# Down-projection weights loaded in rows of 3 KB, up-projection weights read with a column step of three

## The chip, the cores and the metric

The kernel runs on one core of one Trainium2 chip. The metric is the device time in microseconds of one execution. A second execution is recorded by the hardware profiler; its page and its trace are read here.

## What is computed

The reference is a chunked state-space layer (Mamba2 SSD) whose output goes through a bilinear feed-forward layer. Cut to what matters:

```python
# x (4, 8, 768, 32), a (4, 8, 768), B and C (4, 8, 768, 16), all float32; chunk = 32
for c in range(nc):
    cum = np.cumsum(log_a[chunk c], axis=-1)
    M = (Cc @ Bc.T) * exp(cum_i - cum_j) * causal
    y[chunk c] = M @ xc + (Cc @ state) * exp(cum)
    state = exp(sum(la)) * state + sum_j exp(cum_last - cum_j) * Bc[j] (x) xc[j]

X = y.transpose(0, 2, 1, 3).reshape(3072, 256)
out = ((X @ w_a) * (X @ w_b)) @ w_out     # w_a, w_b (256, 1536), w_out (1536, 256)
```

In the bilinear layer the order of the 1536 hidden columns is free, as long as w_a, w_b and the rows of w_out use the same order.

## The kernel before

The sequence of 768 is cut into 6 blocks of Q = 128. Two batches form a pair, so there are NP = 12 pairs of 256 tokens, numbered p = 2 * block + half of the batches. The order of instructions is written out by hand (a manual schedule): each engine runs its own instructions in the order of the Python calls, and the framework adds the semaphore waits that the tiles' reads and writes need. It finds these by comparing the regions that two instructions touch.

For each pair, the attention half does this: `scale` turns B, C and x into f16 with the decay factors (GpSimd, in the beginning VectorE and ScalarE); `transposes` brings B and C to the other orientation; `scores` forms C B in PSUM; `mask` (L319, VectorE) multiplies by the causal mask; `pv` (L328 and L362) adds the part within the block and the part from the state; ScalarE writes the result as f16 to X2T (L374); `state` carries the state on.

The feed-forward half of a pair is six calls of `unit(p, k2)`, each for two of the NK = 12 groups of 128 hidden columns. A unit does four products of `Wa` into one PSUM bank and four of `Wb` into another (L433): two column groups k by two halves f of the 256 inputs. The stationary operand is a 128 x 128 piece of the weights, the moving one is X2T of the pair (256 columns). ScalarE then copies the first bank (asb, L442), and VectorE multiplies it with the second into hk (L443). `out_half(p, bt)` is twelve products of hk with `Wo` (L450), an evacuation and a store of 128 x 256 floats.

All of TensorE's work is in one queue. The first units of up products, unit(0,0), unit(0,1) and unit(0,2), stand between the scores of pair 1 and pv(1). On VectorE the masks of pair 1 and the products hk of pair 0 alternate:

```python
    mask(product(1, 3), by_pool=True)
    for t in range(3):
        load_wo(t)
    h = unit(0, 0)
    mask(product(1, 0))
    h()
    mask(product(1, 1))
    h = unit(0, 1)
    scale_x(1, nc.scalar)
    h()
    mask(product(1, 2))
    go((0, 2))
```

The weights are loaded on GpSimd's queue, with a cast from f32 to f16 during the transfer. `Wa` and `Wb` are tiles of 128 x 2 x 1536; `load_w(half)` (L136) loads columns 0 to 767 or 768 to 1535 of both f of each. Half 0 is issued ahead of everything else on that queue, half 1 after the factors of pair 1; the first unit that uses half 1 is unit(0,3). `load_wo(t)` (L142) loads four of the twelve 128-row groups of w_out, 1 KB rows, one row of each group to a partition. Its three calls stand behind pair 1's mask on GpSimd; behind them stand hr, hs and hsx (L541 to L543), from which TensorE (L552) makes the decays G of the states.

Of the kernel before, what the change touches and what calls it, by code (L numbers as in the profile page):

```python
# [22 lines left out]
def kernel(  # L23
# [13 lines left out]
    nc = tc.nc  # L37
# [43 lines left out]
    Wo = big.tile([128, NK, d_model], f16, name="Wo")  # L81
# [56 lines left out]
        ]  # L138

    def load_wo(t):  # L140
        k = slice(4 * t, 4 * t + 4)
        nc.gpsimd.dma_start(Wo[:, k], moe_w_out.rearrange("(k p) e -> p k e", p=128)[:, k])  # L142

    nc.sync.dma_start(a_sb, a.rearrange("b h (k q) -> (b h) k q", q=Q))
    for p_ in range(3):
# [151 lines left out]
    def product(p, m):  # L297

        return (
            st[p]["T1"][:, 2 * m : 2 * m + 2].rearrange("p e r q -> p e (r q)"),  # L300
            SC[m].rearrange("p (e c) -> p e c", e=2),
        )
# [8 lines left out]
    def mask(out_in, by_pool=False):  # L311
        o_, i_ = out_in
        c_ = causal.rearrange("p r q -> p (r q)").unsqueeze(1).broadcast_to((128, 2, 2 * Q))
        if by_pool:
            tmp = mid.tile([128, 2, 2 * Q], f32, name="tmp", tag="tmp")
            nc.scalar.copy(tmp, i_)
            nc.gpsimd.tensor_tensor(out=o_, in0=tmp, in1=c_, op=ALU.mult)
        else:
            nc.vector.tensor_tensor(out=o_, in0=i_, in1=c_, op=ALU.mult)  # L319
# [103 lines left out]
    def unit(p, k2):  # L423
        s = st[p]
        if k2 == 0:
            s["hk"] = ffh.tile([128, NK, 2 * Q], f16, name="hk", tag="hk")
        a_ps = psf.tile([128, 512], f32, name="aps", tag="ff")
        b_ps = psf.tile([128, 512], f32, name="bps", tag="ff")
        for ps, W in ((a_ps, Wa), (b_ps, Wb)):
            for kk in range(2):  # L430
                k = 2 * k2 + kk
                for f in range(2):
                    nc.tensor.matmul(  # L433
                        ps[:, kk * 2 * Q : (kk + 1) * 2 * Q],
                        W[:, f, k * 128 : (k + 1) * 128],
                        X2T[:, p, f].rearrange("p t q -> p (t q)"),
                        start=(f == 0),
                        stop=(f == 1),
                        skip_group_check=True,
                    )  # L440
        asb = ffh.tile([128, 512], f32, name="asb", tag="asb")
        nc.scalar.copy(asb, a_ps)  # L442
        return lambda: nc.vector.tensor_tensor(  # L443
            out=s["hk"][:, 2 * k2 : 2 * k2 + 2, :].rearrange("p k q -> p (k q)"), in0=b_ps, in1=asb, op=ALU.mult
        )
# [35 lines left out]
    def go(*items):  # L481
        for p, k2 in items:
            unit(p, k2)()
# [43 lines left out]
    v = factors_mm(1, NBLK)  # L527
    nc.scalar.copy(flat(fC, 1, NBLK), v)
    mask(product(1, 3), by_pool=True)
    for t in range(3):  # L530
        load_wo(t)
    h = unit(0, 0)
    mask(product(1, 0))
# [5 lines that stand above are left out]
# [118 lines left out]
```

## Time and profile before

| | |
|---|---|
| device time, median of 3 runs | 134.03 us (132.4 to 134.34) |
| the profiled execution | 132.39 us, span 130.7 us |
| TensorE products (PE) | 122.9 us busy, 94% |
| TensorE weight loads (PEld) | 101.4 us, 78% |
| VectorE (DVE) | 87.3 us, 67% |
| ScalarE (ACT) | 74.5 us, 57% |
| GpSimd (POOL) | 53.5 us, 41% |
| up products, L433 | 576 of 273 ns |
| their weight loads, L433 | 576 of 98 ns |
| down products, L450 | 288 of 273 ns |
| Wo loads, L142 | 3 of 256 KB, 6.2 us from issue to landing (median) |
| mean granted TensorE clock | 0.997 |

The span is the time from the first to the last instruction of the profiled execution; its own device time is 1.7 us more. Products are pipelined: records of 273 ns overlap, so the pace of a series is read from the starts and not from the mean duration. In a line of groups the numbers after the bar are the busy time and the mean of one in ns, then the engine's idle time ahead of them. A line of the timeline has start and duration in us, engine, line, operation, and in square brackets the idle time before it with what ended it. In the chain, TensorE holds 87% of the span.

### The profile page before, as it was taken

To read this page: it belongs to the slowest core of one execution; us is meant where nothing else is said; L and a number is where in the kernel's file an instruction comes from. 1 tells how busy PE (TensorE), PEld (TensorE's weight loads), DVE (VectorE), ACT (ScalarE), POOL (GpSimd) and SP (SyncE) were. 2 spreads that over 40 slices of the span, in tenths; PEclk is the share of its full clock that TensorE was granted. 3 is DMA by queue.
4 is the path that set the end of the run, shared out by engine and by line. 5 is a ranking of instruction groups with operands and counts; after the bars stand their busy time and mean duration, and the time that the engine had idled before them with its cause. 6 is when DMAs were issued, how large, how long until landed. Compare 5 with 4: busy or idle time off the path is not lost.

```text
span 130.7 us, 4724 instructions
## 1 busy us (share of the span) xinstructions
PE 122.9 (94%) x1948; PEld 101.4 (78%) x1948; DVE 87.3 (67%) x161; ACT 74.5 (57%) x153; POOL 53.5 (41%) x76
## 2 busy tenths in 40 slices
PE   6998949989999999999999999999999999999990
PEld 2333938878888888888888888888898888888880
DVE  2786476876693974974975956957939929835441
ACT  3135645795548548556576476576575486455520
POOL 6495486547459607508409319129037000000000
PEclk9999999999999999999999999999999999999998
DMA  3999999931666561542532443614511010110112
GB/s 68 182 122 227 187 189 189 166 89 42 105 138 129 134 148 46 98 105 54 98 100 67 68 111 74 127 50 88 117 46 40 19 60 11 40 40 5 40 40 80
DMA packets 43333, 12.22 MB, mean 94 GB/s; under 512 B 37552, under 2 KB 43216, under 8 KB 43312
## 3 DMA queue, kind: packets, MB, share of 16 engines
q1 hardware_dynamic: 38256, 8.84, 32.4%
q0 software_dynamic: 2800, 2.63, 13.1%
q10 hardware_dynamic: 2256, 0.46, 1.8%
q8 instruction: 15, 0.25, 0.8%
q14 instruction: 6, 0.05, 0.2%
HBM read 11.13 MB, written 3.15 MB: 109 GB/s over the span
## 4 chain that ended last, share of the span: by engine, by line
PE 87%; ACT 5%; DVE 3%; DMA 2%; issue 1%; DVEq 0%
PE aps L433 24%; PE ops L450 23%; PE bps L433 23%; PE SC L286 4%; PE SC L328 3%; PE SC L265 2%; ACT bt L272 2%; PE SC L362 2%; PE tc L195 2%; DMA a_sb<-in_a_dram 2%; PE fps L217 1%; PE SC L345 1%; PE SC L195 1%; DVE t L319 1%; ACT X2T L374 1%
## 5 line engine op out<-in xcount | busy, mean ns | idle before, releaser
L443 DVE TENSOR_TENSOR hk<-bps,asb 128x512 f16<-128x512 f32 x72 | 49.6, 689 | 26.3 <-ACT asb L442 23.8
L442 ACT COPY asb<-aps 128x512 f32<-128x512 f32 x72 | 42.2, 587 | 18.8 <-PE aps L433 17.1
L433 PE MATMUL aps<-X2T,Wa 128*128 128x256 f16 x288 | 43.3, 273 | 0.0
L433 PE MATMUL bps<-X2T,Wb 128*128 128x256 f16 x288 | 43.2, 273 | 0.0
L450 PE MATMUL ops<-Wo,hk 128*128 128x256 f16 x288 | 35.2, 273 | 0.0
L319 DVE TENSOR_TENSOR t<-SC,causal 128x512 f16<-128x512 f32 x46 | 30.3, 682 | 1.6 <-ACT osb L465 0.8
L433 PEld LDWEIGHTS <-Wb 128*128 128x128 f16 x288 | 28.2, 98 | 3.2
L433 PEld LDWEIGHTS <-Wa 128*128 128x128 f16 x288 | 27.2, 98 | 3.9
L450 PEld LDWEIGHTS <-hk 128*128 128x128 f16 x288 | 27.7, 98 | 3.1
L408 POOL TENSOR_TENSOR sbd<-U,maskbd 128x512 f16<-128x512 f32 x10 | 11.6, 1158 | 33.2 <-DVE U L401 31.8
L465 ACT ACTIVATE osb<-ops 128x256 f32<-128x256 f32 x23 | 8.8, 384 | 16.7 <-PE ops L450 16.7
L241 POOL TENSOR_SCALAR x<-xn 128x512 f16<-128x512 f32 x9 | 13.4, 1491 | 1.1 <-DMA xn<-in_x_dram 0.4
L374 ACT ACTIVATE X2T<-SC 128x512 f16<-128x512 f32 x11 | 6.6, 597 | 7.4 <-PE SC L345 6.4
L272 ACT ACTIVATE bt<-SC,ch 128x256 f16<-128x256 f16 x22 | 9.2, 473 | 0.1
L247 POOL TENSOR_TENSOR cm<-cn,fC 128x256 f16<-128x256 f32 x11 | 6.8, 620 | 3.4 <-DMA cn<-in_C_dram 3.4
L401 DVE SCALAR_TENSOR_TENSOR U<-SC,G,gU 128x64 f32<-128x64 f32 x16 | 3.8, 280 | 5.3 <-ACT X2T L374 5.3
L286 PEld LDWEIGHTS <-bt 32*64 32x64 f16 x384 | 3.8, 108 | 4.2 <-issue 3.1
L247 POOL TENSOR_TENSOR bm<-bn,fB 128x256 f16<-128x256 f32 x11 | 6.8, 621 | 0.1
L286 PE MATMUL SC<-ct,bt 32*64 32x128 f16 x384 | 5.4, 227 | 1.3 <-ACT ct L273 1.2
L328 PEld LDWEIGHTS <-x 64*32 64x32 f16 x384 | 3.1, 91 | 4.0 <-issue 2.0
L195 PE MATMUL SC<-warm 128*128 128x512 f16 x10 | 4.8, 629 | 1.2 <-DVE warm L159 1.2
L328 PE MATMUL SC<-t,x 64*32 64x128 f16 x352 | 4.6, 218 | 1.2 <-DVE t L319 1.2
(60 smaller groups left out, 70.6 us busy)
## 6 DMA issues: line engine op xcount, KB each, us to landing
out_dram<-osb SPq DMA_DIRECT2D x23, 128.0 KB, 1.7
xn<-in_x_dram SPq DMA_DIRECT2D x21, 128.0 KB, 3.3
bn<-in_B_dram SPq DMA_DIRECT2D x24, 64.0 KB, 3.0
cn<-in_C_dram SPq DMA_DIRECT2D x21, 64.0 KB, 2.9
Wa<-in_moe_w_a_dram POOLq DMA_DIRECT2D x2, 384.0 KB, 6.1
Wb<-in_moe_w_b_dram POOLq DMA_DIRECT2D x2, 384.0 KB, 7.5
Wo<-in_moe_w_out_dram POOLq DMA_DIRECT2D x3, 256.0 KB, 6.2
xn<-in_x_dram POOLq DMA_DIRECT2D x2, 128.0 KB, 6.9
```

The costliest lines, as they stand in the source:

```text
L241: eng.tensor_scalar(xo, xi, XS, None, ALU.mult)
L247: eng.tensor_tensor(out=m_, in0=pair_in[p][which].rearrange("p h r n -> p r h n"), in1=f[:, blk, :, bp].unsqueeze(3).broadcast_to((128, 2, ...
L272: nc.scalar.activation(out=o_, in_=TB, func=AF.Copy, scale=par[:, e : e + 1])
L286: nc.tensor.matmul(SC[m][64 * bt : 64 * bt + 64, c0 : c0 + Q], BT[rows, e, r, bt], CT[rows, bt], start=True, stop=True, skip_group_check=True,
L319: nc.vector.tensor_tensor(out=o_, in0=i_, in1=c_, op=ALU.mult)
L328: nc.tensor.matmul(py[bt][32 * g : 32 * g + 32, u * Q : (u + 1) * Q], s["X16"][k, h, r, :], s["T1"][k, h, r, :], start=(first and u == 0 a ...
L408: nc.gpsimd.tensor_tensor(out=Sbd.rearrange("p t (m c) -> p t m c", m=4), in0=U32[:, p].unsqueeze(2).broadcast_to((128, 2, 4, 2 * D)), in1 ...
L433: nc.tensor.matmul(ps[:, kk * 2 * Q : (kk + 1) * 2 * Q], W[:, f, k * 128 : (k + 1) * 128], X2T[:, p, f].rearrange("p t q -> p (t q)"), sta ...
L442: nc.scalar.copy(asb, a_ps)
L443: return lambda: nc.vector.tensor_tensor(out=s["hk"][:, 2 * k2 : 2 * k2 + 2, :].rearrange("p k q -> p (k q)"), in0=b_ps, in1=asb, op=ALU.mult)
L450: nc.tensor.matmul(o_ps[:, 0:d_model], hk[:, k, bt * Q : (bt + 1) * Q], Wo[:, k, :], start=(k == 0), stop=(k == NK - 1), skip_group_check= ...
L465: nc.scalar.activation(out=o_sb, in_=o_ps[:, 0:d_model], func=AF.Copy, scale=1.0 / (YS * YS))
```

## The change

Two things change together. The load of w_out takes three consecutive rows to a partition, 3 KB in one piece, in groups of 384 rows; two transfers of six row groups replace three of four. Partition p of slot k then holds row 384 * (k // 3) + 3 * p + k % 3 of w_out. For hidden column and row to match, the up products take as stationary operand every third column of a group of 384, beginning at k % 3, in place of 128 consecutive columns. The loads of Wa and Wb and all other instructions stay as they were.

```diff
     def load_wo(t):
-        k = slice(4 * t, 4 * t + 4)
-        nc.gpsimd.dma_start(Wo[:, k], moe_w_out.rearrange("(k p) e -> p k e", p=128)[:, k])
+        k = slice(6 * t, 6 * t + 6)
+        nc.gpsimd.dma_start(
+            Wo[:, k].rearrange("p (g kk) e -> p g (kk e)", kk=3),
+            moe_w_out.rearrange("(g p kk) e -> p g (kk e)", p=128, kk=3)[:, 2 * t : 2 * t + 2],
+        )
...
                     nc.tensor.matmul(
                         ps[:, kk * 2 * Q : (kk + 1) * 2 * Q],
-                        W[:, f, k * 128 : (k + 1) * 128],
+                        W[:, f, k // 3 * 384 : (k // 3 + 1) * 384].rearrange("p (c kk) -> p kk c", kk=3)[:, k % 3],
                         X2T[:, p, f].rearrange("p t q -> p (t q)"),
...
-    for t in range(3):
+    for t in range(2):
         load_wo(t)
```

## The prediction, made before the changed kernel had run

> **What bounds the kernel now.** I read the page first (busy shares, the chain that ended last, the costliest groups), then the timeline from 5 to 24 us, then the answers on the weight tiles.
>
> ```profile
> span 130.7 us, 4724 instructions
> PE 122.9 (94%) x1948; PEld 101.4 (78%) x1948; DVE 87.3 (67%) x161; ACT 74.5 (57%) x153; POOL 53.5 (41%) x76
> ...
> PE 87%; ACT 5%; DVE 3%; DMA 2%; issue 1%; DVEq 0%
> ...
> L433 PE MATMUL aps<-X2T,Wa 128*128 128x256 f16 x288 | 43.3, 273 | 0.0
> L433 PE MATMUL bps<-X2T,Wb 128*128 128x256 f16 x288 | 43.2, 273 | 0.0
> L450 PE MATMUL ops<-Wo,hk 128*128 128x256 f16 x288 | 35.2, 273 | 0.0
> ```
>
> TensorE is the chain: 87% of the span, busy 94%. The 864 big products run without gaps from about 20 us on; four of them take 0.44 us in the chain, 109 ns each. So there are two ways to move the time: change what one of these products costs, or open a gap in TensorE's queue. The stage before 20 us, where DMA is busy throughout (tenths 9 in seven slices of the page, 3.3 to 26 us), is where gaps are.
>
> The change touches exactly the first unit of up products there, so these lines of the timeline carry the argument:
>
> ```profile
> 9.73 0.74 POOL L136 DMA_DIRECT2D Wa<-in_moe_w_a_dram  x1
> 10.47 0.74 POOL L136 DMA_DIRECT2D Wb<-in_moe_w_b_dram  x1
> ...
> 14.02 0.61 PE L433 MATMUL aps<-X2T,Wa 128*128 128x256 f16 x4
> ...
> 14.47 0.60 PE L433 MATMUL bps<-X2T,Wb 128*128 128x256 f16 x4
> ...
> 15.43 0.69 DVE L443 TENSOR_TENSOR hk<-bps,asb 128x512 f16<-128x512 f32 x1 [1.73 <-ACT asb L442]
> ...
> 17.23 0.68 DVE L319 TENSOR_TENSOR t<-SC,causal 128x512 f16<-128x512 f32 x1
> ...
> 17.97 0.42 PE L328 MATMUL SC<-t,x 64*32 64x128 f16 x32 [1.15 <-DVE t L319]
> ```
>
> The reader is to see the chain unit(0,0) -> hk -> three more DVE operations back to back -> pv(1) at 17.97. The second halves of Wa and Wb are issued at 9.73 and 10.47. The answers on tiles Wa and Wb, restricted to 9 to 12 us, give their landing, counted from issue:
>
> ```profile
> DMA to landing us min/median/max: 7.0/7.0/7.0
> ```
>
> ```profile
> DMA to landing us min/median/max: 8.3/8.3/8.3
> ```
>
> So Wa's second half lands at 9.73 + 7.0 = 16.73 us, Wb's at 10.47 + 8.3 = 18.77 us. In the kernel before nobody notices: the first product that needs them is unit(0,3), after 23 us, and TensorE has no wait on a DMA in the list of waits.
>
> **What the skill says.** The Trainium skill, "SBUF — State Buffer", section "Specifications (TRN2)": cachelines are 16 bytes and two hits per line are needed for full bandwidth. A step of three f16 elements is 6 bytes, two or three hits per line, so by the page the new stationary read runs at full rate. "TensorE: Matmul & The Clock Gate", section "Weight-path perf modes — Fast Weight Load (FWL) and DoubleRow": fast loading takes 128 non-fp32 columns in chunks "packed or strided", with column steps up to 1,024 elements. The trace of before has no strided stationary operand, so it neither confirms nor denies either. The same page, Part 1: TensorE runs at half clock until it has been busy for about 3.4 us and again after an idle window of that length. The trace agrees that there are two speeds: warm-up matmuls of 512 columns came three in 1.46 us at 4.64 us and three in 0.81 us at 11.02 us.
>
> **Part 1, the Wo load.** Three issues of 256 KB become two of 384 KB on POOL (770 ns each, 16.09 to 18.41), so POOL saves 0.77 us, and there are 512 rows of 3 KB where there were 1536 of 1 KB. What follows on POOL is hr, hs, hsx (end 19.19), read by the gps product at 19.45. But gps also stands behind ds_mm(0), released only at 19.27 by X2T on ACT, so the saving ends in a wait. The earlier landing of Wo is worth nothing either: Wo lands by 17.6 + 8.0 = 25.6 us at the latest, its first reader is at 28.80. If that cover were gone the gain would still be at most the 0.26 us between 19.19 and 19.45. Gain: 0.
>
> **Part 2, the stationary step of 3.** 576 weight loads change. A load's record is 98 ns, a product's pace 109 ns. The record isn't the occupancy: the four L362 products (contiguous 128x128 weights, 128 columns) take 0.38 us of records of 219 ns, that is (380 - 219)/3 = 54 ns apart, so a contiguous load needs at most 54 ns of its turn. Under a 256-column product there are 109 ns, so the strided load is free up to twice that. Lower bound 0 (a load cannot become shorter to any profit, it is hidden already). Upper bound: three times as many lines, three times 54 = 162 ns, 53 ns exposed x 576 = 30 us. I take 0, since the page keeps the rate and the cover is 2x.
>
> **Part 3, a wait that the diff does not show.** The compiled order of TensorE's instructions is the same in both, but two semaphore waits sit elsewhere. DMASW5 and DMASW6 are the second halves of Wa and Wb. Before, they are waited for at the first product of unit(0,3) (rows 474 and 482). In the changed kernel, at the second weight load (f = 1) of each half of unit(0,0):
>
> ```
> 249 L436 Ldweights Wa [waits DMASW1]
> 250 L436 Matmult aps<-X2T,Wa 128x256 [waits PE]
> 251 L436 Ldweights Wa [waits DMASW5]
> ...
> 257 L436 Ldweights Wb [waits DMASW2]
> 258 L436 Matmult bps<-X2T,Wb 128x256 [waits PE]
> 259 L436 Ldweights Wb [waits DMASW6]
> ```
>
> The data read are those of the first half; the strided view with f = 1 is evidently taken as overlapping the second-half write (which spans both f). So TensorE issues the first aps product at 14.02, then stands until 16.73; does the other three aps products (0.33 us) and the first bps one; then stands until 18.77. All of TensorE is queued behind: the rest of unit(0,0), unit(0,1), unit(0,2), pv(1).
>
> The step sum: the bps load at 18.77, its product at 18.88, two more at 109 ns, the last starts at 19.10 and ends, with a record of 273 ns, at 19.37; hk about 0.04 later, the lag seen between other products and their reader (20.39 to 20.43 for asb): 19.41. Before it started at 15.43. Delay 3.98 us. The copy asb of this unit, which released hk before, is done by about 17.9 now. Behind hk stand, on DVE in order, t, hk, t; they ran back to back for 2.5 us and still do, because unit(0,1) (another 0.87 us of products plus a 0.59 us copy) is ready at about 20.3, before DVE asks at 20.6. So pv(1), at 17.97, goes to 21.95, and the unbroken TensorE stretch behind it moves as a whole. Nothing later gives it back: between 20 and 127 us TensorE's waits in the profile sum to 0.5 us. DMA before 18.8 us is the same in both kernels (Wo is issued at 16.09 either way, behind the weights on the same queue), so the landing should hold to some 0.5 us.
>
> Sum: 0 + 0 + 3.98 = +4.0 us. The profiled execution took 132.39 us for a span of 130.7, so 136.4 on its terms. It lay at the low end of 132.4 to 134.34; on the median of 134.03 it is 138.0.
>
> **Rivals.**
> A. The stall also cools TensorE. From 14.3 to 18.8 us it would be busy for only some 0.5 us, in gaps of 2.5 and 1.6 us. For: the two speeds above, and the kernel's own warm-up products. Against: no single gap is 3.4 us. The following products would then take twice 109 ns for one window of about 3.4 us: half of that window is lost, 1.7 us, perhaps up to 3 with the gaps at 16 to 19 us in it: 138.0 + 1.7 to 3, about 140.3.
>
> B. The strided load doesn't fit. For: nothing in the trace shows one. Against: the 54 ns above. At 130 ns a load it costs 21 x 576 = 12 us on top (150); at 162 ns 30 us (168).
>
> C. Not slower by what can be told. The place is the idle time of the same stage: TensorE idles 1.15 us ahead of pv(1) and 0.73 us ahead of ds_mm(0). If DVE and ACT used the stall to get ahead, those gaps would close and 3.98 - 1.15 - 0.73 = 2.1 us would remain, 136.1, within 2%. It decides if the masks t of pair 1 run before hk(0,0). Against: DVE takes its instructions in order, and both t stand behind hk(0,0). A landing of Wb before 17.5 us has the same effect; earlier than 14.5 us the time would even be unchanged, 134.0.
>
> D. Faster: the Wo rows free the saturated DMA and something waits less. Part 1 bounds that at 0.26 us, 133.8. It needs the wait of part 3 not to bind.
>
> **How the numbers follow.** Forecast (138.0, within 136.4 to 139): 0.57. A: 0.20. B: 0.11. C: 0.10. D: 0.02. Two per cent is 2.7 us, about what a measurement of this kernel can tell from no change. Slower: forecast, A and B, 0.88; same: C and half of D, 0.11; faster 0.01. The range leaves out B and half of C: 135.6 to 141.5.
>
> **What would show it.** In the changed profile: TensorE waiting in unit(0,0) on DMA Wa and Wb, about 2.5 and 1.6 us; hk's first instance near 19.4; pv(1) near 22; up products still 109 ns apart; weight-load records of the up products anywhere from 98 to about 130 ns without effect; Wo's landing earlier and unread. Wrong if no DMA wait stands there, if the products' pace rises (B), or if the products after the stall show records well over 273 ns (A).

## The result, and the profile after

The changed kernel takes 137.89 us (137.62 to 138.02), the kernel before 134.04 us (132.4 to 134.34) beside it: a ratio of 1.031, 95% interval 1.023 to 1.040. Executions of the kernel before lie mostly near 132.2 or near 134.1 us, so that its median hangs on how many of each were drawn (134.04 of 4 here, 132.46 to 133.51 of 27 to 55 in the comparisons below), and the ratios are therefore ratios of means without the executions more than 1.5% above the fastest of their kernel. Against the lower ones the 3.9 us here are about 5.7 us.

The page after, in the same rows as before (its line numbers are three higher: L433 is L436):

```profile
span 135.9 us, 4723 instructions
...
PE 124.3 (91%) x1948; PEld 105.2 (77%) x1948; DVE 87.3 (64%) x161; ACT 74.6 (55%) x153; POOL 52.7 (39%) x75
...
PE 81%; DMA 9%; POOL 3%; ACT 2%; issue 1%; SPq 1%; DVE 0%; POOLq 0%
...
L436 PE MATMUL aps<-X2T,Wa 128*128 128x256 f16 x288 | 44.8, 279 | 2.9 <-DMA Wa<-in_moe_w_a_dram 2.9
L436 PE MATMUL bps<-X2T,Wb 128*128 128x256 f16 x288 | 44.5, 278 | 1.1 <-DMA Wb<-in_moe_w_b_dram 1.1
L453 PE MATMUL ops<-Wo,hk 128*128 128x256 f16 x288 | 35.2, 273 | 0.0
L436 PEld LDWEIGHTS <-Wa 128*128 128x128 f16 x288 | 29.2, 105 | 6.2 <-DMA Wa<-in_moe_w_a_dram 3.1
```

TensorE has fallen from 87% to 81% of the chain, and DMA has risen from 2% to 9%. In the groups, aps and bps had no idle time before; now they have 2.9 us that ended with DMA Wa and 1.1 us that ended with DMA Wb. The down products keep 273 ns and no idle time. The means of 279 and 278 ns for the up products are the first sign that some of them ran slower than 273. A weight load of the up products is 105 ns in the mean, 98 before.

The timeline after shows the place:

```profile
13.76 0.29 PE L436 MATMUL aps<-X2T,Wa 128*128 128x256 f16 x1
...
15.84 1.48 POOL L142 DMA_DIRECT2D Wo<-in_moe_w_out_dram  x2
...
16.97 0.82 PE L436 MATMUL aps<-X2T,Wa 128*128 128x256 f16 x3 [2.92 <-DMA Wa<-in_moe_w_a_dram]
...
17.59 0.42 PE L436 MATMUL bps<-X2T,Wb 128*128 128x256 f16 x1
...
19.11 0.82 PE L436 MATMUL bps<-X2T,Wb 128*128 128x256 f16 x3 [1.10 <-DMA Wb<-in_moe_w_b_dram]
...
19.73 1.06 PE L436 MATMUL aps<-X2T,Wa 128*128 128x256 f16 x4
20.04 0.69 DVE L446 TENSOR_TENSOR hk<-bps,asb 128x512 f16<-128x512 f32 x1 [6.60 <-PE bps L436]
...
20.58 1.06 PE L436 MATMUL bps<-X2T,Wb 128*128 128x256 f16 x4
...
23.09 0.42 PE L331 MATMUL SC<-t,x 64*32 64x128 f16 x32
...
24.90 0.62 PE L436 MATMUL aps<-X2T,Wa 128*128 128x256 f16 x4
```

One aps product at 13.76, then nothing until 16.97; three aps and one bps product, then nothing until 19.11. hk starts at 20.04 (15.43 before), pv(1) at 23.09 (17.97). And the products are slow: four take 0.85 us from start to start (19.73 to 20.58), 213 ns each and not 109. TensorE's clock has dropped, as a stretch of 2 us shows (busy us of PE, PEld, DVE, ACT, POOL, then TensorE's clock, here 0.50, the DMA share and GB/s):

```profile
20.00:22.00 2.00, 2.00 (x11) 1.45 (x10) 1.54 (x3) 1.11 (x2) 0.00 (x0) 0.50 1.19 219
```

The trace's record of the granted clock has it at half from 15.93 to 22.76 us. It fell 1.9 us after the first gap began. By 24.90 a series of four has its old 0.62 us.

The answers on Wa and Wb, restricted to 9 to 12 us, give the landing of the second halves, from issues at 9.8 and 10.6 us:

```profile
DMA to landing us min/median/max: 7.1/7.1/7.1
```

```profile
DMA to landing us min/median/max: 8.5/8.5/8.5
```

Wa is there at 16.9, Wb at 19.1 us, the moments at which TensorE goes on. TensorE waits for data that it doesn't read: unit(0,0) uses columns 0 to 383, which are all in the first half.

### The profile page after: what moved, and what is told of

It reads as the page before. It is cut to its first block, busy times and chain, and to the rows that moved or that the text cites. A ratio compares the mean times of both kernels' runs of the same rounds, so it can differ in the third digit from the quotient of the medians.

```text
span 135.9 us, 4723 instructions
## 1 busy us (share of the span) xinstructions
PE 124.3 (91%) x1948; PEld 105.2 (77%) x1948; DVE 87.3 (64%) x161; ACT 74.6 (55%) x153; POOL 52.7 (39%) x75
## 4 chain that ended last, share of the span: by engine, by line
PE 81%; DMA 9%; POOL 3%; ACT 2%; issue 1%; SPq 1%; DVE 0%; POOLq 0%
PE aps L436 24%; PE bps L436 24%; PE ops L453 22%; DMA Wb<-in_moe_w_b_dram 6%; PE SC L331 3%; PE SC L289 3%; DMA bn<-in_B_dram 3%; PE SC L268 2%; PE SC L365 2%; PE SC L348 1%; POOL Wa L136 1%; ACT bt L275 1%; ACT X2T L377 1%; POOL xn L122 1%; POOL Wb L136 1%
## 5 line engine op out<-in xcount | busy, mean ns | idle before, releaser
L436 PE MATMUL aps<-X2T,Wa 128*128 128x256 f16 x288 | 44.8, 279 | 2.9 <-DMA Wa<-in_moe_w_a_dram 2.9
L436 PE MATMUL bps<-X2T,Wb 128*128 128x256 f16 x288 | 44.5, 278 | 1.1 <-DMA Wb<-in_moe_w_b_dram 1.1
L436 PEld LDWEIGHTS <-Wa 128*128 128x128 f16 x288 | 29.2, 105 | 6.2 <-DMA Wa<-in_moe_w_a_dram 3.1
L436 PEld LDWEIGHTS <-Wb 128*128 128x128 f16 x288 | 30.1, 105 | 3.9 <-DMA Wb<-in_moe_w_b_dram 1.6
L244 POOL TENSOR_SCALAR x<-xn 128x512 f16<-128x512 f32 x9 | 13.4, 1490 | 1.2 <-DMA xn<-in_x_dram 0.5
L276 ACT COPY ct<-SC 128x256 f16<-128x256 f16 x11 | 5.0, 455 | 0.0
```

The lines of the kernel that those rows point to most:

```text
L244: eng.tensor_scalar(xo, xi, XS, None, ALU.mult)
L436: nc.tensor.matmul(ps[:, kk * 2 * Q : (kk + 1) * 2 * Q], W[:, f, k // 3 * 384 : (k // 3 + 1) * 384].rearrange("p (c kk) -> p kk c", kk=3)[ ...
```

## The experiments

**A tile for each half of the weights.** The whole change stays; only the tiles differ, so that no view of one half can touch the other.

```diff
-    Wa = big.tile([128, 2, d_ff], f16, name="Wa")
+    Wa = [big.tile([128, 2, d_ff // 2], f16, name=f"Wa{i}") for i in range(2)]      # Wb likewise
...
-            nc.gpsimd.dma_start(W[:, :, c], src...)
+            nc.gpsimd.dma_start(W[half], src...)
...
-                        W[:, f, k // 3 * 384 : (k // 3 + 1) * 384].rearrange(...)[:, k % 3],
+                        W[k // 6][:, f, k % 6 // 3 * 384 : (k % 6 // 3 + 1) * 384].rearrange(...)[:, k % 3],
```

> The whole change is kept (column step of three, Wo in 3 KB rows), but each half of Wa and of Wb has a tile of its own, so that the first unit's weight loads can only wait for the half they read. Theory W (the loss is the wait for the second halves, with the clock that it costs): no wait on a DMA in unit(0,0), first hk back near 15.4 us, about 134 us, the time of before. Theory S (the strided weight load itself costs): the loss stays, about 138 us, or at least 1 us of it. The load records should be 103 ns as in the changed kernel, the pace of the products 109 ns. If the 3 KB rows bring anything, it is seen here as a time under that of before, by at most 0.3 us.

Measured: 133.76 us (132.05 to 134.52, 22 runs), ratio to before 1.004 (1.000 to 1.008). No wait in TensorE's list ends with DMA Wa or Wb. The timeline of this kernel:

```profile
14.23 0.62 PE L436 MATMUL aps<-X2T,Wa 128*128 128x256 f16 x4
...
14.69 0.60 PE L436 MATMUL bps<-X2T,Wb 128*128 128x256 f16 x4
...
15.64 0.69 DVE L446 TENSOR_TENSOR hk<-bps,asb 128x512 f16<-128x512 f32 x1 [1.73 <-ACT asb L445]
...
18.18 0.42 PE L331 MATMUL SC<-t,x 64*32 64x128 f16 x32 [1.14 <-DVE t L322]
```

The two stalls are gone, hk is at 15.64, pv(1) at 18.18. So the loss was the wait, with the clock that it cost, all but 0.4% of the time of before; the step of three as such isn't it. The median is 1.2 us above that of the 27 executions of before beside it (132.59 us), in the main since more of these executions lost clock: 13 of 22 have a mean granted clock below 0.99, against 12 of 27. These counts are too close to call it an effect of the kernel.

The profiled execution, at 133.55 us, kept its clock at 1.00 and was held by something else:

```profile
PE SC L268 <- POOL cm L250: 0.7, 1, 0.7
```

That is pair 2's C: GpSimd waited 2.58 us for its DMA and scaled it only at 25.52 us. So the times above 133 us are not all of one kind.

**The wait alone.** The kernel before, consecutive columns and all, with the two waits put in by hand.

```diff
-        load_w(1)
+        w1 = load_w(1)
...
-                    nc.tensor.matmul(
+                    mm = nc.tensor.matmul(
...
+                    if (p, k, f) == (0, 0, 1):
+                        tc.add_manual_dep(mm.ins, w1[W is Wb].ins.name, AFTER, reason="second half of the weights")
```

> The kernel before (128 consecutive columns, Wo in three loads), with the second products (k = 0, f = 1) of unit(0,0) made to wait for the second halves of Wa and Wb, at the same two places as in the changed kernel. Theory W: 137.9 us, as the changed kernel, with TensorE waiting on DMA Wa some 2.9 us and on DMA Wb some 1.1 us. Theory S: a part of the loss is missing, 137 us or less.

Measured: 137.75 us (136.96 to 138.25), ratio 1.040 (1.032 to 1.048): the changed kernel's time without its change. Its list of waits on TensorE:

```profile
PE aps L433 <- DMA Wa<-in_moe_w_a_dram: 2.8, 1, 2.8
...
PE bps L433 <- DMA Wb<-in_moe_w_b_dram: 1.1, 1, 1.1
```

The same two stalls, 2.8 and 1.1 us (2.9 and 1.1 in the changed kernel). Together with the first experiment this is taking the cause away and putting it back.

**The stalls filled with warm-up products.** To split the loss into the wait and the clock.

```diff
         for ps, W in ((a_ps, Wa), (b_ps, Wb)):
+            if p == 0 and k2 == 0:
+                warmup(14 if W is Wa else 7, ps)
```

> The changed kernel, with 14 warm-up products of 512 columns ahead of the aps products and 7 ahead of the bps products of unit(0,0), written to banks that the unit's own products then start anew; at 0.21 us each they fill 2.9 and 1.5 us of the two stalls. If the drop of the clock after the stall costs what the trace suggests (pv(1) 5.1 us late, of which the wait itself explains 4.3 to 4.6), the time falls by 0.5 to 1 us, to about 137.2, and the up products after the stall come 109 ns apart instead of 213. If the drop is of no consequence: 137.9. If the filling is too long and delays the unit: up to 138.5.

Measured: 136.86 and 137.02 us with a mean granted clock of 0.999 and 1.000, 138.67 and 138.9 us with 0.987 and 0.988; the median of 137.84 is that of the changed kernel. The profiled execution took 136.86 us:

```profile
14.14 3.19 PE L198 MATMUL aps<-warm 128*128 128x512 f16 x14
...
17.17 0.60 PE L438 MATMUL aps<-X2T,Wa 128*128 128x256 f16 x4
...
17.61 1.67 PE L198 MATMUL bps<-warm 128*128 128x512 f16 x7
...
19.11 0.60 PE L438 MATMUL bps<-X2T,Wb 128*128 128x256 f16 x4
...
19.82 0.69 DVE L448 TENSOR_TENSOR hk<-bps,asb 128x512 f16<-128x512 f32 x1 [6.00 <-PE bps L438]
...
22.36 0.42 PE L331 MATMUL SC<-t,x 64*32 64x128 f16 x32 [0.90 <-DVE t L322]
```

The unit's products go 109 ns apart again (0.60 us for four, not 1.06), pv(1) stands at 22.36 and not 23.09, and the span is 135.1 us and not 135.9. Against the kernel before, pv(1) is 22.36 - 17.97 = 4.4 us late. Not all of this is the wait: the filling outlasts it. The answer on Wb in this profile, restricted to 9 to 12 us, gives the landing of its second half, issued at 10.65 us:

```profile
DMA to landing us min/median/max: 8.0/8.0/8.0
```

So the half is there at 18.7 us, while the unit's products with Wb start at 19.11, behind the last warm-up product. About 0.4 us of the 4.4 is therefore filling, and 4.0 us is the wait. In the changed kernel that half landed 0.4 us later, at 19.1. There the wait alone would thus also come to about 4.4 us, and the rest of its 5.1 us (23.09 - 17.97), 0.7 us, is what the lost clock cost; the spans give 0.8. These are estimates from single profiles. The two executions 1.8 us higher have no profile, but their lower clock points to another loss of clock; what such a step is in the kernel before, the next experiment shows.

**The kernel before once more, and its own lost clock.**

> The kernel before, unchanged, once more under the profiler. Its first profile had TensorE at full clock throughout (132.4 us), while most of its first runs took 134 us. Theory C: the longer executions of it lose the clock of TensorE for one window after the two gaps ahead of pv(1) and of ds_mm(0) (idle 1.15 and 0.73 us), as the profile of the step of six shows (products 213 ns apart from 20.2 to 23 us, 134.25 us). Then a profile at 134 us shows products 213 ns apart near 20 us, and one at 132.4 doesn't. Theory D: late inputs of pair 2; then the profile at 134 us shows GpSimd waiting for DMA cn and TensorE waiting ahead of the transposes of pair 2.

Measured: 132.04 and 134.04 us; the profiled one was that of 134.04, with a span of 132.3 us. Stretches of 2 us from 20 to 24 us, first of the profile shown at the beginning, then of this one:

```profile
20.00:22.00 2.00, 2.00 (x21) 1.79 (x19) 1.58 (x6) 1.23 (x3) 1.35 (x2) 1.00 1.41 202
22.00:24.00 2.00, 2.00 (x21) 1.80 (x19) 1.69 (x3) 1.25 (x3) 2.00 (x4) 1.00 1.34 182
```

```profile
20.00:22.00 2.00, 2.00 (x14) 1.49 (x12) 1.55 (x5) 0.63 (x3) 1.38 (x2) 0.60 1.41 198
22.00:24.00 2.00, 2.00 (x12) 1.39 (x11) 0.69 (x1) 0.88 (x2) 2.00 (x4) 0.54 1.37 192
```

Clock 1.00 in one, 0.60 and 0.54 in the other; 42 products in these 4 us in one, 26 in the other. Up to 20 us the two agree within 0.03 us (unit(1,0) at 19.78 and 19.75). TensorE does not wait for pair 2's C here. So an execution of the same program keeps or loses the clock after the two gaps ahead of pv(1) and ds_mm(0), and this costs 1.6 us of span (132.3 against 130.7).

The traces also record when the clock changed. Here it is at half from 20.42 to 23.83 us, for 3.41 us; in the changed kernel for 6.83 us, twice that. In all the traces the stretches between two changes are whole multiples of 3.41 us (10.24, 6.83 and 112.64 us in the changed kernel; 10.24, 3.41 and 109.23 here), counted from a moment that differs from execution to execution. Where this grid falls against the two gaps may decide which executions lose the clock; no run tested that.

**Those gaps filled.** The version that the finding points to, on the kernel before:

```diff
+    warmup(4, SC[0])
     pv(1)
+    warmup(3, SC[0])
     ds_mm(0, 320)
```

> The kernel before, with four warm-up products of 512 columns ahead of pv(1) and three ahead of ds_mm(0), written to a score bank that is free there; at 0.21 us each they fill 0.85 of the 1.15 us and 0.64 of the 0.73 us that TensorE idles. Theory C: no half clock near 20 us, nearly all times near 132.3 us, the median 0.7 to 1.5 us under that of before. Theory D, or a fill that delays pv(1): no change, or 0.2 us more.

Measured: 132.19 us (131.85 to 132.75, 22 runs), beside it before with 132.46 (131.86 to 134.13, 43 runs), 18 of these over 133 us and none of the filled ones. The ratio of 0.998 (0.996 to 1.000), which leaves the upper times of before out, hardly tells the two apart; it is the upper times that are gone.

```profile
16.14 1.02 PE L195 MATMUL SC<-warm 128*128 128x512 f16 x4
...
17.34 0.42 PE L328 MATMUL SC<-t,x 64*32 64x128 f16 x32 [0.17 <-DVE t L319]
...
17.84 0.82 PE L195 MATMUL SC<-warm 128*128 128x512 f16 x3
```

The gap of 1.15 us ahead of pv(1) is 0.17. The fill delays nothing: from the first hk to pv(1) it is 2.54 us in both profiles, from pv(1) to unit(1,0) 1.80 and 1.81. Two of the 22 executions (132.34 and 132.67 us) have a mean granted clock of 0.986 all the same, so they lost clock in some place where it cost little.

**The change with half tiles and filled gaps.** The same seven products on the first experiment's kernel.

> The step of three and 3 KB rows with a tile for each half of the weights, and the same seven warm-up products. Theory C: as the kernel before with the gaps filled, within 0.3 us, about 132.4 us: the loss of the change gone, and the clock kept. The step of three may cost 0.1 us over the whole kernel (an iteration of the pair loop took 9.39 us with it, 9.38 without).

Measured: 132.62 us (132.0 to 133.8), ratio 1.002 (0.999 to 1.004). The loss of the change is gone, and the mean granted clock is 0.996 or more in 21 of 22 executions (0.987 in the one at 133.8 us). But it stays 0.4 us over the filled kernel with consecutive columns, both against the same runs of before. The pair loop explains little of it: from the first unit of its first pass to that of its last it takes 75.0 us (33.38 to 108.37) and 74.9 in the filled kernel (32.76 to 107.67). In the two profiles, with spans of 130.8 and 130.1 us, the whole difference already stands where unit(0,0) starts (14.08 and 13.39 us), ahead of the first strided load; from unit(1,0) to the end both take 111.0 us. In the profiles without the added wait that start lies anywhere from 13.4 to 14.3 us; what moves it was not settled.

**Only the rows of Wo.** The kernel before with the two loads of 3 KB rows.

```diff
-    for t in range(3):
+    for t in range(2):                 # load_wo as in the change; the up products as before
         load_wo(t)
```

> The kernel before with only the loads of Wo changed to two of 3 KB rows; the up products keep consecutive columns, so that hidden columns and rows of w_out are paired in another order and the output is not the reference's. Theory W: within 0.3 us of before, 134.0, since Wo isn't waited for in either. A theory in which the faster transfer of Wo helps the loads behind it: 133 or less.

Measured: 132.7, 133.97, 134.09 and 134.32 us, ratio 1.010 (1.002 to 1.019), with a span of 131.0 us in the profiled execution against 130.7. Three of the four lost clock (0.987 in the mean, against 1.000 in the one at 132.7), so they can't show a loss of 1%; what they do show is that there is no gain of a microsecond. GpSimd did save its time (two issues in 1.48 us, three in 2.32 before), and it went where the prediction put it: into a wait. In this profile hsx is done by 18.7 us, and its reader, gps, starts at 19.75, right behind ds_mm(0).

**Longer steps.** Every sixth column within half tiles, and every twelfth in whole tiles, with the rows of Wo loaded in the order that each needs.

```diff
-                        W[:, f, k // 3 * 384 : (k // 3 + 1) * 384].rearrange("p (c kk) -> p kk c", kk=3)[:, k % 3],
+                        W[k // 6][:, f].rearrange("p (c kk) -> p kk c", kk=6)[:, k % 6],       # step of six
+                        W[:, f].rearrange("p (c kk) -> p kk c", kk=12)[:, k],                  # step of twelve
```

> As the kernel with a tile for each half, but with a column step of six (every sixth column of a half, 12 bytes) and Wo in rows of 6 KB. It measures what a longer step costs a weight load, apart from any wait. The skill's line rule gives one or two hits per 16-byte line instead of two or three: a penalty, if it applies to this read. Theory H (a load stays hidden as long as its turn fits under 109 ns): load records from 103 up to perhaps 120 ns, pace still 109 ns, time as the step of three, 132 to 134.5 us. Theory S: records and pace rise together, 0.576 us for each ns that the pace rises over 109.

> The changed kernel with a column step of twelve (24 bytes, at most one element of a line) and Wo in rows of 12 KB, in whole tiles, so that the first unit must wait for the second halves as in the changed kernel. Theory H: 138 us like the changed kernel, pace 109 ns, load records perhaps 110 to 150 ns. Theory S: at one line per element the load no longer fits under a 256-column product; at a pace of 130 ns the time is 12 us longer, 150 us.

Measured: 133.8 us (132.22 to 134.78, 20 runs; ratio 1.001, 0.997 to 1.005) with the step of six; 139.53 us (138.73 to 140.66, 4 runs; ratio 1.046, 1.035 to 1.056) with the step of twelve. There TensorE waits at the same unit, 3.7 and 1.1 us, but this wait is a real one: every twelfth of 1536 columns lies in both halves, so that already the first product reads the second. The weight loads of Wa with steps of 3, 6 and 12, minimum, median and maximum in ns:

```profile
L436 PEld LDWEIGHTS <-Wa x288: 102/103/153, 13.8 to 129.2; 128*128 128x128 f16 x144
```

```profile
L436 PEld LDWEIGHTS <-Wa x288: 124/125/152, 13.9 to 125.8; 128*128 128x128 f16 x144
```

```profile
L436 PEld LDWEIGHTS <-Wa x288: 138/143/169, 17.5 to 130.4; 128*128 128x128 f16 x144
```

A record grows from 98 (consecutive) to 103, 125 and 143 ns. The pace of the products doesn't follow. In the kernel with a step of twelve:

```profile
41.10 0.60 PE L436 MATMUL aps<-X2T,Wa 128*128 128x256 f16 x4
...
41.54 0.60 PE L436 MATMUL bps<-X2T,Wb 128*128 128x256 f16 x4
```

Four products in 0.44 us, 109 ns each, below a load record of 143 ns. The loads overlap, and a record is not the time that a load takes of its turn. Theory S is out for all three steps, though a small cost is left: the pair loop takes 74.9, 75.0, 75.1 and 75.3 us with steps of 1, 3, 6 and 12, at most 0.35 us in eight passes. With the step of twelve the profiled execution (138.77 us) has a span 1.1 us above the changed kernel's: 0.8 of it stands already at unit(1,0) (25.70 against 24.90), behind the longer wait, and 0.3 comes in the pair loop. The two executions at 140.29 and 140.66 us have a mean granted clock of 0.948, against 0.971 and 0.975 in the other two; they lost more clock.

**Wo later.** An attempt to make room for pair 2's inputs, on the kernel before and on the half tiles with the step of three:

```diff
-    for t in range(3):
-        load_wo(t)
...
     scale_bc(2, 1, nc.gpsimd)
+    for t in range(3):                 # two with the 3 KB rows
+        load_wo(t)
```

> The kernel before with the three Wo loads moved behind the factors of pair 2 on GpSimd (from 16 to about 23.5 us). The times of the kernel before lie around 132.2 and around 134.1 us; in one profile at 133.6 us pair 2's C came late, landing after 11 us, and TensorE waited 0.7 us for it. If the Wo traffic of 16 to 24 us is what holds pair 2's C up, the upper group goes and the median is 132.2 or less. If it isn't, both groups stay. If Wo then lands after its first reader at 28.8 us, TensorE waits there for DMA Wo and the time rises by 0.5 to 2 us.

> The step of three and the 3 KB rows, a tile for each half of the weights, and the two Wo loads behind the factors of pair 2. The 3 KB rows land sooner than the 1 KB rows, if packets count: then this is the best of both, 132.0 us with one group of times, and no wait for Wo at 28.8 us, where the kernel with 1 KB rows at the same place has one or a smaller margin. If rows don't count: the same time as with the 1 KB rows.

Measured: 134.68 us (133.72 to 138.29, 20 runs; ratio 1.014, 1.011 to 1.017) and 135.04 us (133.47 to 138.11, 20 runs; 1.013, 1.010 to 1.017). Both lost, and the profiles show the risk that was named:

```profile
PE ops L450 <- DMA Wo<-in_moe_w_out_dram: 1.1, 2, 0.8
```

```profile
PE ops L453 <- DMA Wo<-in_moe_w_out_dram: 1.3, 1, 1.3
```

TensorE now waits for Wo, 1.1 us with 1 KB rows and 1.3 with 3 KB rows. The longer rows land hardly sooner where it would have counted: the last of them 7.6 us after the first issue, the last of the 1 KB rows 7.8. The waits for Wo are not all of the loss, since 17 and 16 of the 20 executions have a mean granted clock below 0.99. The times spread over 4 us and more, and with a new wait in both kernels they can't tell whether pair 2's inputs matter. What does tell is in the profiles above: at 134.04 us C was on time and the clock was lost, at 133.55 us C was late and the clock was kept.

## Why the prediction was right

It said 138.0 us and a wait for the second halves of Wa and Wb; it was 137.89 us and that wait. Step by step:

- The Wo load, 0 predicted: held. GpSimd's saving and the earlier landing had nobody waiting for them; the rows alone brought no gain.
- The stationary step of 3, 0 predicted from 54 ns against 109: held for the pace. The record rose by 5 ns only, as the Trainium skill's rule of two hits per line suggests ("SBUF — State Buffer", section "Specifications (TRN2)"), and by 27 and 45 ns at steps that have fewer. The upper bound of 30 us (three times the lines, three times the occupancy) was far too careful: even twelve columns apart, with a load record of 143 ns, nothing of it was exposed in a series. Rival B, that the load doesn't fit, did not happen.
- The wait, read from the compiled order: held, in place and in kind. Landing at 16.9 and 19.1 us for 16.73 and 18.77 predicted. Shown by taking it away (half tiles) and by putting it into the kernel before. The two stalls were 2.9 and 1.1 us where 2.5 and 1.6 were named, since unit(0,0) began 0.26 us earlier, Wa landed 0.2 us later, and the slow products filled part of the second.
- Its size: held. With the stalls filled, and the landing of Wb at 18.7 us as predicted, it is about 4.0 us once the filling is taken off. In the changed kernel Wb landed 0.3 us later than predicted, and the lost clock came on top.
- The three DVE operations behind hk, "back to back for 2.5 us": failed. They took 3.0 us, because unit(0,1) ran at half clock and VectorE waited for its bps bank (0.42 us at 21.75).
- Rival A, given 0.20 as a case of its own: it happened, together with the forecast. The sign that the prediction named for it, records well over 273 ns behind the stall, is there (421 ns at most), and all four executions have a mean granted clock of 0.973 or 0.975. The reason against it ("no single gap is 3.4 us") did not hold, as the clock fell 1.9 us into the first gap. Its price of 1.7 to 3 us was too high: some 0.7 to 0.8 us is what it cost. Of the 6.83 us at half rate TensorE stood idle for a part, and some of the slow products went into the 1.15 us that it had idled ahead of pv(1).
- The median of 134.03 as base: it held a loss of the clock of its own. Against the profile at full clock the span grew by 5.2 us (130.7 to 135.9), that is about 4.0 for the wait, 0.3 to 0.4 for the later landing and 0.8 for the clock. Against the executions of before that lose the clock anyway, 1.6 us later, it is 3.6 (132.3 to 135.9). The sum of 4.0 agreed with 3.85 measured because the clock is missing on both of its sides: left out of the cost, and left out of the base. The mechanism was right; the agreement to 0.1 us was luck.
- Rival C, not slower since the gaps ahead of pv(1) absorb the stall: did not happen. VectorE kept its order, and the gap ahead of ds_mm(0) stood as before (0.73 us). The gap ahead of pv(1) did close, but under slow products and not by work done in advance. Rival D, a gain from the rows: none was seen.

Why the framework sees an overlap only in the strided view with f = 1 was not tried. Wa's second half is written as columns 768 to 1535 of both f, so the span from its first to its last element holds all of f = 1's first half; that it compares such spans for a strided view, and exact regions for a plain one, is an inference.

## What to carry to other kernels

Compare the compiled order with its waits, not only the diff: a view that steps through its elements can inherit a wait on a transfer of elements that it doesn't read, and a tile for each transfer removed it here, at a cost of less than 1%. Ask of a longer weight load whether the pace of the products follows, and not how long its record is. Before an idle gap of a microsecond or two on TensorE is called free, look whether the products behind it keep their pace; where the gap is known, a few dummy products into a free bank can hold the clock, as seven did here. Fill no longer than the wait lasts: 0.4 us of filling too much was 0.4 us of delay.

## What the runs showed of the hardware

- TensorE can lose half its clock after two gaps of 1.15 and 0.73 us within 3 us, in some executions of a program and not in others, and 1.9 us into a single gap of 2.9 us. The Trainium skill ("TensorE: Matmul & The Clock Gate", Part 1) speaks of an idle window of about 3.4 us; here no gap was that long. The half rate itself lasted 3.41 us in the kernel before (20.42 to 23.83 us, at a cost of 1.6 us) and 6.83 us in the changed one, and all stretches between changes of the clock were multiples of 3.41 us. With seven products of 512 columns in the gaps none of 22 executions was over 132.8 us; without them 18 of 43 were over 133.
- The record of a 128 x 128 f16 weight load grows with the column step: 98, 103, 125 and 143 ns at 1, 3, 6 and 12. Under 256-column products the pace within a series stays at 109 ns in all four.
- 768 KB of weights in two transfers of 3 KB rows landed 7.6 us after the first issue, in three of 1 KB rows 7.8 us (GpSimd's late loads, one profile each).
